# Where the first experts' weights are asked for: two 256 KB loads in each fifth convolution slot instead of one load beside nearly every block of x

## The chip, the cores and the metric

The kernel runs on one core of one Trainium2 chip. The metric is device time in microseconds (us). A core has engines that work side by side: TensorE (PE; its weight loads are listed apart as PEld), VectorE (DVE), ScalarE (ACT), GpSimd (POOL) and SyncE (SP). All loads and stores of this kernel are DMAs that SP issues in the order of its own instruction stream; sixteen DMA engines carry them out.

## What is computed

A convolution with weights that differ by token and head, followed by a soft mixture of experts. All data are float32.

```python
def _attn_ref(x, weight_gen):              # x [8, 3584, 192], weight_gen [8, 3584, 8 heads, 7 taps]
    w = softmax(weight_gen, axis=-1)       # over the 7 taps
    x_pad = concatenate([zeros(B, 6, D), x], axis=1)
    x_unf = x_pad[:, idx, :].reshape(B, S, 7, H, 24)
    return einsum('bshk,bskhg->bshg', w, x_unf).reshape(B, S, D)

def _moe_ref(x, phi, w1, w2):              # x [28672, 192], w1 [8, 192, 1024], w2 [8, 1024, 192]
    logits = x @ phi                       # 8 experts of 4 slots: 32 columns
    d = softmax over tokens (axis 0) of logits
    slot_input = (d.T @ x).reshape(8, 4, 192)
    slot_out[e] = relu(slot_input[e] @ w1[e]) @ w2[e]
    c = softmax over slots (axis 1) of logits
    return c @ slot_out
```

## The kernel before

The tokens are cut into 280 groups of 104. A **slot** `k` (0 to 69) is one call of `convs(k)`: the convolution of four groups on TensorE (64 matmuls of line 274), with ScalarE copying the result out of PSUM. Around it come six transposes per pair of groups (line 293) and, once per four slots, a **unit**: the logits (lines 345 and 349), their running maximum, the exponentials and the dispatch matmuls (line 425). VectorE, GpSimd and ScalarE turn the tap weights into the banded matrices (`band`) that the convolution multiplies with; they also do the softmax over slots (`soft`) for the tokens that are done.

After slot 69 there is a short chain: the rest of the last unit, then `hidden` (line 917, experts' first layer, reads `w1a_sb` and `w1b_sb`), `outputs` (line 934, second layer, reads `w2`), and then the output rows (line 996, copied at line 1005, stored at line 1012).

What SP loads, and when:

- `loadx` (line 170): a block of x, 32 partitions by 960 elements, 120 KB. Four of them make one x tile `t` (0 to 55) of five groups. `feed(k)` asks for tile `t + 4` in the slot in which tile `t` is used for the last time, `(5t + 4) // 4 == k`. So 480 KB of x are asked for in four slots of five, and none where `k` is a multiple of five.
- `loadw` (line 173): the tap weights (`wh`) of eight groups, 182 KB, once per two slots.
- `loadw1` (line 495): a piece of the first experts' weights, into `w1a_sb` or `w1b_sb`; these tiles have no other use before the output rows. A piece is 256 columns, 128 KB; with `n = 2` it is 512 columns, 256 KB. There are 48 pieces, 6.3 MB.
- `loadw2` (line 502): the second experts' weights, 256 KB each, into the memory of x tiles that are no longer needed.

`feed` only lists the operations. A planner (`model`, `times`) simulates the engines with the costs given in `op`, and the instructions are emitted in the order of the planned starts; on PE and SP the listed order is kept. Every DMA planned later than 24 us is held back by `paced`: SP waits for the PE instruction that stands at the same planned time. So SP's queue follows TensorE's progress.

Before the change, `feed` puts `loadw1` behind the x of a tile: 6 loads of 256 KB with tiles 3, 5, 7, 9, 12 and 14, then 30 loads of 128 KB with tiles 16 to 49 (seven tiles of eight), then 6 more of 128 KB beside the first `loadw2`.

Of the kernel before, what the change touches and what calls it, by code (L numbers as in the profile page):

```python
# [30 lines left out]
NS, E, SE, F = 32, 8, 4, 1024  # L31
# [2 lines left out]
TAIL = 4  # L34
PACED = 24.0
LEAD, LATE = 9, 4.6
WLATE, WPAIRS = 42, 12
FILL = 2
WGAP = 0.9
TR = 3 * 32 + T  # L40
# [22 lines left out]
def conv_soft_moe(ctx, tc, xh, wh, phi, w1a, w1b, w2a, w2b, out):  # L63
# [190 lines left out]
    def unit(p):  # L254
        return next((u, p - p0) for u, (p0, n) in enumerate(UNITS) if p < p0 + n)
# [257 lines left out]
    def op(eng, cost, reads, writes, f, *a, late=0.0, due=None):  # L513


        i = len(ops)
        preds = {writer[r] for r in (*reads, *writes) if r in writer}
        for r in writes:
            preds |= set(readers.get(r, ()))
            writer[r], readers[r] = i, []  # L520
        for r in reads:
            readers.setdefault(r, []).append(i)
        preds.discard(i)
        ops.append((eng, cost, late + 0.1 * (eng == "TE"), preds, due, f, a))
# [4 lines left out]
    def x_all(t):  # L529
        return [x_of(t, h) for h in range(4)]  # L530

    def loadxs(t, cost, late, hs=(0, 2, 1, 3)):
        for h in hs:
            op(SP, cost, [], [x_of(t, h)], loadx, t, h, late=late)
# [17 lines left out]
    VE, AC, PO, TE, SP = "VE", "AC", "PO", "TE", "SP"  # L552
# [113 lines left out]
    def feed(k):  # L666
        for c in range(3, NCH):
            if k == max(0, CH * c - 4):
                chain(c)
        for c in range(6, NCH):  # L670
            if k == CH * c - LEAD - (c > 9):
                op(SP, 0.5, [], [("w", c % NTAP, b) for b in range(CH)], loadw, c, late=LATE)
        for t in range(NSG):
            if (SGG * t + SGG - 1) // 4 == k:
                if t + NXS < NSG:
                    loadxs(t + NXS, 0.52, 3.0)
                else:
                    i = t + NXS - NSG
                    for j in range(WLATE + 3 * i, min(WLATE + 3 * (i + 1), 4 * (E + E // 2))):
                        op(SP, 0.5, [], [], loadw1, j)  # L680
                    freed = True
                    for j, (b, o, n) in enumerate(W2S):
                        if i == (W2B * b + o + n - 1) // XB:
                            op(SP, WGAP, [] if freed else x_all(t), x_all(t) if freed else [],
                               loadw2, j)
                            freed = False
                for j in range(WLATE):
                    n = 1 if j >= WPAIRS else 2 - j % 2 * 2
                    if n and 3 + j * 8 // 7 == t:
                        op(SP, 0.15 + 0.3 * n, [], [], loadw1, j, n)  # L690
        for c in range(NTAP, 6):
            if k == CH * c - 7 - c % 2:
                op(SP, 0.5, [], [("w", c % NTAP, b) for b in range(CH)], loadw, c, late=LATE)

    v = final - 1
    for k in range(SLOTS):
        u, i = unit(2 * k)[0], unit(2 * k)[1] // 2
        if u == final and i == 0:
            op(PO, 0.2, [], [("wide", b) for b in range(CH)]
               + [(*tm_of(x), j) for x in (k, k + 1) for j in range(2)], edges, [NTM], G)  # L700
        convs(k)
        if 0 < k < UP // 2 + 1:
            xposes(k - 1)
        feed(k)
        if i == 0 and u > 1:
            xposes(k - 2, k - 1)
        elif i == 1 and u > 0:
            slots(u - 1)
        elif i == 2 and u > 0:
            settle(u - 1)  # L710
            xposes(k - 2, k - 1)
        elif i == 3 and u > 0:
            ends(u - 1)
            saves(u - 1)
    k = SLOTS - 2
# [125 lines left out]
    for i in sorted(range(len(ops)), key=lambda i: (at[i], i)):  # L841
        if ops[i][5] is loadw2 and ops[i][6] in later:
            continue
        n = len(block.instructions)
# [356 lines left out]
```

## Time and profile before

| | |
|---|---|
| median of 3 timed runs | 287.76 us (286.5 to 290.84) |
| profiled execution, device time | 288.77 us |
| its span, first to last instruction | 286.6 us |
| TensorE busy | 256.9 us, 90% of the span |
| DMA engines busy (queue q1, data) | 73.6% of 16 engines' span |
| slots 0 to 69 | from 8 to about 210 us |
| last rows stored | from about 230 us to the end |

The page gives busy times per engine and a line of tenths in 40 slices. The slices show two parts: in the first three quarters TensorE is at 9 tenths in nearly every slice while the DMA engines stand at 5 to 9 tenths; in the last part the DMA engines are at 9 tenths and move about 420 GB/s. "Issue" as the reason of an idle time means that the engine waited for nothing that the profile shows. A DMA that SP issues is listed under SPq. Instruction fetches have DMA queues of their own (q8 and q14, "instruction").

### The profile page before, as it was taken

To read this page: it belongs to the slowest core of one execution; us is meant where nothing else is said; L and a number is where in the kernel's file an instruction comes from. 1 tells how busy PE (TensorE), PEld (TensorE's weight loads), DVE (VectorE), ACT (ScalarE), POOL (GpSimd) and SP (SyncE) were. 2 spreads that over 40 slices of the span, in tenths; PEclk is the share of its full clock that TensorE was granted. 3 is DMA by queue.
4 is the path that set the end of the run, shared out by engine and by line. 5 is a ranking of instruction groups with operands and counts; after the bars stand their busy time and mean duration, and the time that the engine had idled before them with its cause. 6 is when DMAs were issued, how large, how long until landed. Compare 5 with 4: busy or idle time off the path is not lost.

```text
span 286.6 us, 15079 instructions
## 1 busy us (share of the span) xinstructions
PE 256.9 (90%) x6520; PEld 200.9 (70%) x6520; DVE 211.6 (74%) x375; ACT 177.8 (62%) x296; POOL 161.5 (56%) x257
## 2 busy tenths in 40 slices
PE   8899989999999999999999999999999998899000
PEld 4688878888888988878898898898966743232000
DVE  8788888888867769978898899977357698954000
ACT  8887456765666577656776767757540089988100
POOL 9987848674567368488669798673312017530000
PEclk9999999999999999999999999999999999968655
DMA  5777976676765777758757667656889389999995
GB/s 173 213 200 222 255 226 195 179 217 195 230 200 150 217 222 213 208 164 237 203 178 209 196 205 231 187 177 191 258 284 301 111 316 417 420 429 427 419 429 225
DMA packets 28240, 69.69 MB, mean 243 GB/s; under 512 B 5648, under 2 KB 14992, under 8 KB 27024
## 3 DMA queue, kind: packets, MB, share of 16 engines
q1 hardware_dynamic: 28176, 68.75, 73.6%
q8 instruction: 51, 0.84, 1.2%
q14 instruction: 13, 0.11, 0.1%
HBM read 46.68 MB, written 22.04 MB: 240 GB/s over the span
## 4 chain that ended last, share of the span: by engine, by line
PE 78%; POOL 5%; DMA 4%; DVE 2%; ACT 2%; issue 2%; ACTq 0%; SPq 0%; POOLq 0%; DVEq 0%
PE ring L274 34%; PE ring L293 16%; PE acb L425 8%; PE two L996 5%; PE ls L345 4%; PE ls L349 4%; DMA out<-w1b_sb 2%; PE ring L917 2%; PE acb L373 2%; DMA out<-w1a_sb 1%; POOL big L441 1%; PE ring L934 1%; POOL LT L103 1%; ACT w1a_sb L1005 1%; POOL taps L205 1%
## 5 line engine op out<-in xcount | busy, mean ns | idle before, releaser
L274 PE MATMUL ring<-big,band 128*26 128x96 f32 x4480 | 109.4, 248 | 2.6 <-issue 1.3
L274 PEld LDWEIGHTS ring<-big,band 128*26 128x26 f32 x4480 | 99.3, 130 | 11.9 <-issue 6.4
L281 ACT COPY tm<-ring 128x768 f32<-128x768 f32 x68 | 54.4, 800 | 59.7 <-PE ring L274 59.6
L245 DVE STREAM_TRANSPOSE band<-wide 128x832 f32<-128x832 f32 x70 | 69.8, 1022 | 6.4 <-POOL wide L236 4.6
L293 PE MATMUL ring<-ident,tm 122*128 122x122 f32 x408 | 50.0, 272 | 0.8 <-issue 0.8
L293 PEld LDWEIGHTS ring<-ident,tm 122*128 122x128 f32 x408 | 43.7, 144 | 3.3 <-issue 0.8
L299 ACT COPY cm<-ring 128x624 f32<-128x624 f32 x68 | 44.0, 689 | 2.0 <-PE ring L293 2.0
L236 POOL TENSOR_TENSOR wide<-taps,sum 128x364 f32<-128x364 f32 x32 | 31.4, 982 | 16.8 <-DVE band L245 10.8
L205 POOL TENSOR_TENSOR taps<-taps,top 128x364 f32<-128x364 f32 x34 | 33.1, 976 | 8.8 <-DVE top L197 8.7
L221 POOL TENSOR_TENSOR si<-taps 128x208 f32<-128x208 f32 x34 | 21.7, 638 | 16.0 <-ACT taps L213 15.5
L197 DVE TENSOR_REDUCE top<-taps 128x52 f32<-128x364 f32 x34 | 27.8, 819 | 1.7 <-DMA taps<-wh 1.5
L425 PE MATMUL acb<-tm,dt 128*32 128x193 f32 x544 | 25.9, 328 | 0.5 <-issue 0.4
L103 POOL TENSOR_TENSOR LT<-LT,rm 128x576 f32<-128x576 f32 (+1 forms) x16 | 18.1, 1136 | 9.9 <-DVE rm L101 9.9
L115 POOL TENSOR_TENSOR LT<-LT,sm 128x576 f32<-128x576 f32 (+1 forms) x16 | 18.0, 1135 | 9.9 <-DVE sm L113 9.9
L996 PE MATMUL two<-cT,so 32*128 32x468 f32 (+4 forms) x136 | 20.8, 596 | 1.4 <-ACT w1a_sb L1005 0.8
L425 PEld LDWEIGHTS acb<-tm,dt 128*32 128x32 f32 x544 | 16.9, 110 | 4.1 <-issue 0.6
L355 DVE TENSOR_REDUCE mx<-ls 128x1 f32<-128x416 f32 x17 | 10.1, 592 | 12.8 <-PE ls L349 12.8
L213 ACT ACTIVATE taps<-taps 128x364 f32<-128x364 f32 (+1 forms) x36 | 18.1, 503 | 1.8 <-POOL taps L205 1.7
L227 DVE RECIPROCAL sum<-sum 128x52 f32<-128x52 f32 (+1 forms) x36 | 16.5, 457 | 3.2 <-POOL sum L223 3.0
L996 PEld LDWEIGHTS two<-cT,so 32*128 32x128 f32 x136 | 8.5, 196 | 12.6 <-ACT w1a_sb L1005 6.0
L1005 ACT COPY big<-two 128x936 f32<-128x936 f32 (+2 forms) x18 | 14.9, 910 | 0.8 <-PE two L996 0.7
L222 POOL TENSOR_TENSOR si<-si 128x104 f32<-128x104 f32 x34 | 13.9, 408 | 2.7
(140 smaller groups left out, 307.8 us busy)
## 6 DMA issues: line engine op xcount, KB each, us to landing
big<-xh SPq DMA_DIRECT2D x224, 120.0 KB, 3.4
out<-big SPq DMA_DIRECT2D x5, 1794.0 KB, 13.0
taps<-wh SPq DMA_DIRECT2D x35, 182.0 KB, 3.5
big<-w2a SPq DMA_DIRECT2D x16, 256.0 KB, 3.8
out<-w1b_sb SPq DMA_DIRECT2D x2, 1794.0 KB, 12.1
out<-w1a_sb SPq DMA_DIRECT2D x2, 1794.0 KB, 14.4
w1a_sb<-w1a SPq DMA_DIRECT2D x20, 128.0 KB, 3.5
w1b_sb<-w1b SPq DMA_DIRECT2D x16, 128.0 KB, 3.4
```

What stands on the lines that cost most here:

```text
L103: G.tensor_tensor(out=lt, in0=lt, in1=rms.pop(h).to_broadcast([128, n, NS]), op=ALU.subtract)
L197: V.tensor_reduce(out=row(m), in_=run(c, 0, KT).rearrange("p k s -> p s k"), axis=AX.X, op=ALU.max)
L205: eng.tensor_tensor(out=t, in0=t, in1=rows7(tops.pop((c, 0))), op=ALU.subtract)
L221: eng.tensor_tensor(out=fold, in0=run(c, 0, 4), in1=run(c, 4, 8), op=ALU.add)
L236: eng.tensor_tensor(out=dst, in0=raw[c % NTAP][:, 0:KT], in1=m.unsqueeze(1).to_broadcast([128, KT, n, T]), op=ALU.mult)
L245: V.transpose(bands[c % NBAND][:, b].rearrange("p b j l -> p (b j l)"), wide[:, b].rearrange("p b j -> p (b j)"))
L274: P.matmul(to, bands[g // 8 % NBAND][:, g // 4 % CH, :, i], xbd[:, place(t), :, b * GW : (b + 1) * GW].rearrange("p h (a i) -> p h a i", i ...
L281: copy(tms[tm_at(u)][:, pr + of.start : pr + of.stop, 1 : 2 * D + 1], cv[:, of, 0 : 2 * D])
L293: P.transpose(pt[:, j // 3, o : o + TR], tm[0:TR, pr + j // 3, 1 + o : 129 + o], ident[0:TR, 0:TR])
L299: copy(cm.rearrange("p (a i) (b j) -> p a (i b) j", i=3, j=T), pts["t", k][:, of, 0 : 3 * 128].rearrange("p a (i j) -> p a i j", j=32)[... ...
L425: P.matmul(ac[32 * q : 32 * q + 32], dt[:, g, :], tm[:, g // 2, o : o + D + 1], start=(g < 4), stop=(g + 4 >= 2 * n))
L996: P.matmul(pos[j][q // 2][m * half : m * half + m, q % 2, 0 : widths(g, n)[q]], of[32 * q : 32 * q + 32], cT[32 * q : 32 * q + 32, g0 : g0 ...
```

## The change

The lines of `feed` that tie `loadw1` to the x tiles are taken out, with their two constants. In their place, each slot `k` that is a multiple of five (the slots in which no x is asked for), from slot 10 to slot 65, lists two `loadw1` of 256 KB: 24 loads in 12 slots. The planner's cost for one is 0.75 us, as it was before for a load of 256 KB.

```diff
-WLATE, WPAIRS = 42, 12
...
                 else:
                     i = t + NXS - NSG
-                    for j in range(WLATE + 3 * i, min(WLATE + 3 * (i + 1), 4 * (E + E // 2))):
-                        op(SP, 0.5, [], [], loadw1, j)
                     freed = True
...
-                for j in range(WLATE):
-                    n = 1 if j >= WPAIRS else 2 - j % 2 * 2
-                    if n and 3 + j * 8 // 7 == t:
-                        op(SP, 0.15 + 0.3 * n, [], [], loadw1, j, n)
+        if k % 5 == 0:
+            for j in range(4 * (k // 5 - 2), 4 * (k // 5 - 1), 2):
+                if 0 <= j < 4 * (E + E // 2):
+                    op(SP, 0.75, [], [], loadw1, j, 2)
```

The order on TensorE is the same row for row. On VectorE, GpSimd and ScalarE some steps of `soft` change places with their neighbours. The large difference is on SP, at three places. (The kernel of the change has three lines less, so its line 169 is line 170 of before, and so on.)

SP near the start, before (`big<-xh` is x, `taps<-wh` the tap weights, `128x512` of `w1a` a 256 KB load):

```order
L170 DMA big<-xh 32x960 x8
L495 DMA w1a_sb<-w1a 128x512
L173 DMA taps_81<-wh 128x364
L170 DMA big<-xh 32x960 x4
L173 DMA taps_78<-wh 128x364
L170 DMA big<-xh 32x960 x4
L495 DMA w1a_sb<-w1a 128x512
L170 DMA big<-xh 32x960 x4
L173 DMA taps_79<-wh 128x364
L170 DMA big<-xh 32x960 x4
L495 DMA w1a_sb<-w1a 128x512
```

SP at the same place, after:

```order
L169 DMA big<-xh 32x960 x8
L172 DMA taps_81<-wh 128x364
L169 DMA big<-xh 32x960 x4
L172 DMA taps_78<-wh 128x364
L169 DMA big<-xh 32x960 x8
L172 DMA taps_79<-wh 128x364
L169 DMA big<-xh 32x960 x4
L172 DMA taps_80<-wh 128x364
L494 DMA w1a_sb<-w1a 128x512 x2
```

The first two w1 loads have left this stretch; the first pair of the change stands behind the same six x tiles as the third 256 KB load before.

SP in the middle of the convolutions, before (`128x256` of `w1a` or `w1b` is a load of 128 KB):

```order
L495 DMA w1b_sb<-w1b 128x256
L170 DMA big<-xh 32x960 x4
L495 DMA w1b_sb<-w1b 128x256
L173 DMA taps_78<-wh 128x364
L170 DMA big<-xh 32x960 x4
L495 DMA w1a_sb<-w1a 128x256
L170 DMA big<-xh 32x960 x4
L495 DMA w1a_sb<-w1a 128x256
L173 DMA taps_79<-wh 128x364
L170 DMA big<-xh 32x960 x4
L495 DMA w1a_sb<-w1a 128x256
L173 DMA taps_80<-wh 128x364
```

SP between the same tap loads, after:

```order
L494 DMA w1b_sb<-w1b 128x512 x2
L172 DMA taps_81<-wh 128x364
L169 DMA big<-xh 32x960 x8
L172 DMA taps_78<-wh 128x364
L169 DMA big<-xh 32x960 x8
L172 DMA taps_79<-wh 128x364
L494 DMA w1a_sb<-w1a 128x512 x2
L169 DMA big<-xh 32x960 x4
L172 DMA taps_80<-wh 128x364
```

Where every x tile had a w1 load beside it, two tiles now follow each other with a tap load at most, and the w1 loads come in pairs with a tap load next to them.

SP at the end of the convolutions, before:

```order
L170 DMA big<-xh 32x960 x8
L495 DMA w1b_sb<-w1b 128x256 x3
L502 DMA big<-w2a 128x512 x7
L495 DMA w1b_sb<-w1b 128x256 x3
L502 DMA big<-w2a 128x512 x9
L502 DMA big<-w2b 128x512 x8
```

and after:

```order
L169 DMA big<-xh 32x960 x8
L494 DMA w1b_sb<-w1b 128x512 x2
L169 DMA big<-xh 32x960 x16
L494 DMA w1b_sb<-w1b 128x512 x2
L501 DMA big<-w2a 128x512 x16
L501 DMA big<-w2b 128x512 x8
```

The last six w1 loads no longer stand between the loads of the second experts' weights.

## Rows read from the trace of the kernel before

**Rows 1.** Busy time, slots 2 to 69: us, busy (x instructions) per engine, PEclk, DMA share, GB/s.

```profile
13.40:209.60 196.20, 193.63 (x5707) 168.39 (x5707) 159.93 (x278) 129.26 (x226) 133.30 (x215) 1.00 0.71 206
```

**Rows 2.** TensorE's waits, 13.4 to 209.6 us, all of them: us, times, longest.

```profile
PE ring L274 <- issue: 1.3, 4, 0.4
PE ring L293 <- issue: 0.8, 1, 0.8
PE ring L274 <- DVE band L245: 0.5, 1, 0.5
PE acb L425 <- issue: 0.4, 1, 0.4
```

**Rows 3.** Chain that ended last, in order: start us, us, what.

```profile
21.70 0.70 PE ls L345 x8
...
33.73 0.70 PE ls L345 x6
...
46.54 0.70 PE ls L345 x8
...
92.54 0.70 PE ls L345 x8
...
103.87 0.70 PE ls L345 x8
...
208.22 0.70 PE ls L345 x8
...
228.76 0.60 PE two L996 x8
```

**Rows 4.** TensorE in order of time: start us, us, line, operation, [idle before <- releaser].

```profile
32.68 0.56 PE L274 MATMUL ring<-big,band 128*26 128x96 f32 x16 [0.33 <-issue]
...
37.53 0.68 PE L293 MATMUL ring<-ident,tm 122*128 122x122 f32 x5 [0.77 <-issue]
...
42.45 0.79 PE L274 MATMUL ring<-big,band 128*26 128x96 f32 x25 [0.24 <-issue]
...
124.21 0.41 PE L274 MATMUL ring<-big,band 128*26 128x96 f32 x9 [0.42 <-issue]
```

**Rows 5.** DMA queues, 13.4 to 209.6 us: packets, MB, share of 16 engines.

```profile
q8 instruction: 45, 0.74, 1.6%
```

**Rows 6.** DMA queues, 34.9 to 36.1 us.

```profile
q8 instruction: 1, 0.02, 6.0%
```

**Rows 7.** DMA queues, 33.0 to 34.9 us.

```profile
q1 hardware_dynamic: 242, 0.52, 92.9%
```

**Rows 8.** SP's issues in order of time, two stretches: start us, us, line, what.

```profile
25.02 1.25 SPq L495 DMA_DIRECT2D w1a_sb<-w1a  x1
...
32.30 0.35 SPq L495 DMA_DIRECT2D w1a_sb<-w1a  x1
...
38.39 0.37 SPq L495 DMA_DIRECT2D w1a_sb<-w1a  x1
...
119.03 0.37 SPq L495 DMA_DIRECT2D w1b_sb<-w1b  x1
119.57 0.35 SPq L173 DMA_DIRECT2D taps<-wh  x1
```

**Rows 9.** Busy time, 27 to 36 us, columns as in the first group.

```profile
27.00:36.00 9.00, 8.67 (x281) 7.77 (x273) 7.82 (x13) 4.93 (x8) 7.90 (x15) 1.00 0.92 257
```

**Rows 10.** DMA issues, 13.4 to 209.6 us: KB each, median us to landing.

```profile
big<-xh SPq DMA_DIRECT2D x208, 120.0 KB, 3.5
taps<-wh SPq DMA_DIRECT2D x31, 182.0 KB, 3.6
w1a_sb<-w1a SPq DMA_DIRECT2D x6, 256.0 KB, 4.0
```

**Rows 11.** DMA queues, 59.9 to 61.5 us.

```profile
q1 hardware_dynamic: 194, 0.44, 82.9%
q8 instruction: 1, 0.02, 5.0%
```

## The prediction

> **What bounds the kernel now.** I first read the busy times of the convolution part as one stretch. Of its 196.2 us TensorE is busy 193.6, while the DMA engines are busy 0.71 of the time [rows 1]. So loads as such do not bound this part; TensorE does, at a granted clock of 1.00, which is its upper level (2.4 GHz). Its waits come next. No entry in the list is a DMA of x, taps or w1; nearly all of it is "issue": 1.3 + 0.8 + 0.4 us in six pieces, in which TensorE waited for nothing that the profile shows [rows 2].
>
> The chain of work that ended last shows what those pieces cost. A unit of four slots starts with the logits of line 345. A quiet unit lasts 103.87 - 92.54 = 11.33 us. From the first listed start to the last, 208.22 - 21.70 = 186.52 us pass, which is 16 units; at 11.33 us they would take 181.28. So 5.24 us in all are lost, in some of the units [rows 3]. The first two are such: 12.03 us (0.70 too long) and 12.81 us (1.48 too long). TensorE in order of time shows the pieces in the middle of a run of equal matmuls, for instance 0.77 us up to 37.53 and 0.42 us up to 124.21 [rows 4]. The first unit holds one piece (up to 32.68), the second two, so one costs 0.70 to 0.74 us of unit time, more than its idle in most rows (0.24 to 0.77). I call it a stall. The remaining three of the six waits come after 103.87 us, where nine units take 208.22 - 103.87 = 104.35 us, 2.38 more than 9 x 11.33: 0.79 each. The four units from 46.54 to 92.54 lose 46.00 - 45.32 = 0.68 us without a listed wait of TensorE.
>
> What are they? In this part the instruction queue q8 carries 45 packets [rows 5], while TensorE starts 5707 matmuls and 5707 weight loads [rows 1]: 11414 / 45 = 254 instructions per packet. So q8 is TensorE's code, a block each 4.4 us. A packet runs between 34.9 and 36.1 us [rows 6], the stall ends at 37.53. In the 1.9 us before that packet the data queue kept the DMA engines busy to 92.9% [rows 7]. My reading: behind much data a code block is fetched late, and TensorE runs dry.
>
> The Trainium skill, "Runtime: NRT & Kernel Launch", section "Instruction fetch mechanics", says that code is refilled in 16 KiB blocks of 256 instructions (the trace agrees: 254) and that crossing a block costs a DMA step that is "mostly hidden". Here six of 45 are not. By the rule taken strictly the stalls are something else and the change leaves the time as it is; that is the first rival below.
>
> **The change, part by part.** The bytes stay: 6.3 MB of w1. Only when they are asked for changes, and in which size. TensorE's order is the same, so every term is a stall more or less.
>
> *How full a slot is.* A slot lasts 11.33 / 4 = 2.83 us. At a DMA share of 0.92 the queues moved 257 GB/s [rows 9], so full engines move 280 GB/s here, or 0.79 MB per slot. Demands by the sizes issued [rows 10]: x 4 x 120 KB = 0.49 MB, taps 0.19 MB in every second slot, w1 0.13 or 0.26 MB. Before: x, taps and a 128 KB w1 make 0.81 MB (1.02 of a slot); with a 256 KB w1 0.94 MB (1.19); x and w1 0.62 (0.79). After: x and taps 0.68 (0.85), x alone 0.49 (0.62); the fifth slot with its pair 0.52 (0.66), with taps 0.71 (0.90). No slot is overfull any more.
>
> *First stretch, to 46.5 us.* Before, 256 KB loads are issued at 25.02, 32.30 and 38.39 us [rows 8], and the first two stalls lie within 8 us of the first two. In the change both are gone and the first pair stands where the third load was. I take two stalls away, 0.70 + 0.74 = 1.44 us; the third, up to 42.45, stays, since a pair is now close to it.
>
> *After 46.5 us.* 0.68 + 2.38 = 3.06 us are lost there. Ahead of the stall at 124.21, w1 and taps are issued back to back (119.03, 119.57) between x tiles [rows 8]. The change takes w1 out of the x slots, but puts 0.52 MB in a row once in five slots (14.2 us, against a code block each 4.4 us). I count half of the loss as gone: 1.53 us.
>
> *New stalls beside the twelve pairs.* Until the x loads end, the trace shows no two w1 loads in a row. The bound below is none (a pair fills 0.66 to 0.90 of its slot). The bound above is one stall at each pair: 12 x 0.70 = 8.4 us. I take one, 0.70 us, nearer the lower bound, since three of the six 256 KB loads [rows 10] come after the three just named, and the four units from 46.54 us on show no stall.
>
> *Work that the change costs at nothing.* (a) 24 issues instead of 42: SP's issues take 0.35 to 0.38 us where nothing holds them [rows 8], and SP waits for TensorE anyway. (b) A 256 KB load of w1 landed 4.0 us after its issue [rows 10]; the last pair is asked for in slot 65, four slots or 11 us before the last slot ends, and w1 is first read after that. (c) x behind a pair: 0.52 MB at 280 GB/s hold it up by 1.9 us; x is asked for one tile turn ahead of three others, 3.75 slots or 10.6 us before use, against 3.5 us of landing. Taps are asked for still earlier. If that cover were gone, each late x would cost TensorE up to 1.9 us. (d) The steps of `soft` that change places on the other engines: they delay a `band` by one such step at most; the waits list names bands with 0.5 us, once [rows 2]. (e) At the end, six w1 loads leave the stretch of the w2 loads. The chain from 208.22 to the first output rows at 228.76 [rows 3] names no load, so I give this nothing; the stores behind it keep their length.
>
> *Sum.* -1.44 - 1.53 + 0.70 = -2.3 us. Against the profiled execution: 288.8 - 2.3 = 286.5 us (span 286.6 - 2.3 = 284.3). That execution is 1.0 us above the median of the runs shown, so against the median, 287.76 - 2.3 = 285.5 us.
>
> **The rivals.**
>
> *No change.* The stalls come when they come, or the load does not decide. For it: a code packet between 59.9 and 61.5 us met 82.9% of data load and no stall followed [rows 11]. Against it: the first two stalls lie where the slots are fullest (1.19). Time: 287.8 us. Another page would give the same: the Trainium skill, "DMA: Bandwidth & Descriptors", section "Queues, rings and completion order", says that a DMA engine takes turns between its queues packet by packet, so that code would wait for one data packet and not for a backlog; the trace neither shows nor excludes that, as the rows name no queue depth.
>
> *Nearly all stalls go.* If the overfull slots alone cause them, 4.6 (the six) to 5.24 us are won: 282.5 to 283.2 us. Against it: 0.90 of a slot stays, and 82.9% is not far from 92.9%.
>
> *Slower: a pair starves code.* Two loads of 256 KB in a row put 0.52 MB before a code block that comes then; with taps beside them 0.71 MB, or 2.5 us of transfer, more than half of the 4.4 us between blocks. If each pair stalls TensorE once: 8.4 us more and at most 5.2 less, 291.0 us. It is slower from the eighth stall at pairs on (5.24 / 0.70 = 7.5), and by over 2% (5.8 us) only if a pair costs (5.8 + 5.2) / 12 = 0.92 us each.
>
> *The change doesn't do what it says*: the planner could have moved the pairs to other places. SP's order shows them between taps and x as described, so I give this none.
>
> **How the numbers follow.** Some stalls go (1 to 3.5 us won): 50%. Nearly all go: 15%. No change within 1 us: 22%. Slower by 1 to 5.7 us: 10%. Slower by more: 3%. The likeliest gives **285.5 us**. The range leaves out most of the slower cases (above 1.4 us of loss) and the last third of "nearly all go": **282.8 to 289.2 us**. A measurement of this kernel can tell about 2% (5.8 us) from no change. Faster by that is more than all the time lost in the convolutions (5.24 us), so only an error in the reading gives it: 0.04. Slower by that: 0.03. Within: 0.93.
>
> **What would show it.** In the profile after, the units of the first stretch should last 11.3 to 11.6 us, where they lasted 12.03 and 12.81; the data queue should stay below nine tenths there; TensorE's "issue" waits should fall from 2.5 us to about 1.5 us in three or four pieces; the output part should keep its length and start 2 us earlier. The prediction is wrong if the pieces stay as many with the load evened out (then load is not the cause), if they gather behind the pairs, or if TensorE begins to wait for x or taps.

## The result: the change costs 0.8%, and where the time went

The changed kernel takes 289.67 us (median of 14 timed runs, 288.78 to 292.12), the kernel before, timed beside it, 287.72 us (14 runs, 286.5 to 291.12). The ratio is 1.0076, 95% interval 1.0049 to 1.0103. On another chip the same two kernels later gave 290.44 against 288.78 us, ratio 1.0032 (0.9996 to 1.0068). So it is slower by 0.3 to 0.8%, where 0.8% faster was forecast, and the time lies outside the range. The ratios here leave out runs that are over 1.5% above the fastest of the same kernel, so they can differ a little from the quotient of the medians.

The profiled execution took 291.1 us, its span is 289.1 us, 2.5 more than the span of before. Lines of the kernel after are one lower up to about line 500 (L273 is L274 of before).

Busy times of the changed kernel by stretch: us, busy (x instructions) of TensorE, its weight loads, VectorE, ScalarE, GpSimd, then the granted clock, DMA share, GB/s:

```profile
13.40:46.60 33.20, 33.20 (x1014) 28.73 (x1018) 29.36 (x45) 22.59 (x41) 25.38 (x50) 1.00 0.74 218
46.60:209.60 163.00, 158.18 (x4628) 137.42 (x4624) 129.68 (x234) 105.76 (x184) 107.84 (x165) 1.00 0.67 201
```

```profile
13.40:212.00 198.60, 193.78 (x5706) 167.88 (x5706) 159.66 (x278) 129.15 (x226) 133.68 (x215) 1.00 0.69 205
```

The same matmuls (5706 against 5707) are busy for the same time as before (193.78 against 193.63 us), at the same granted clock of 1.00; but they need 198.60 us where they needed 196.20 [rows 1]. TensorE never pauses up to 46.6 us. It pauses later, 4.8 us in 163, with the DMA engines less busy than before. So it is no lack of bandwidth on average.

TensorE's waits, 13.4 to 212 us, all of them (us, times, longest):

```profile
PE ring L273 <- issue: 3.3, 6, 0.9
PE acb L372 <- DVE top L196: 0.9, 1, 0.9
PE ls L344 <- ACT taps L212: 0.6, 1, 0.6
PE ring L273 <- DVE band L244: 0.5, 1, 0.5
```

"Issue" was 2.5 us in six pieces before [rows 2] and is 3.3 us in six pieces. Two entries are new, with 1.5 us together. They name VectorE and ScalarE, but what the two matmuls read was written over a microsecond before they started at 71.86 and 117.37 us: `mq` until 70.62, `cm` until 116.02 (start us, us, what):

```profile
70.40 0.22 DVE L356 TENSOR_SCALAR mq<-acb,mx 128x4 f32<-128x4 f32 x1
...
114.71 1.31 ACT L298 COPY cm<-ring 128x624 f32<-128x624 f32 x2
```

So I count them as stops of the same kind; the last section has a second reason.

The chain that ended last, at the starts of units (start us, us, what):

```profile
21.78 0.70 PE ls L344 x8
33.11 0.70 PE ls L344 x8
44.59 0.70 PE ls L344 x8
56.95 0.70 PE ls L344 x7
...
104.24 0.70 PE ls L344 x8
117.37 0.91 PE ls L344 x8
...
210.86 0.70 PE ls L344 x8
```

The first two units take 11.33 and 11.48 us where they took 12.03 and 12.81 [rows 3]: this gain came. Then it turns. The third unit takes 12.36 us, the one from 104.24 even 13.13. From 21.78 to 210.86 us the 16 units take 189.08 us, which is 7.80 above 16 x 11.33 (5.24 before). The rest of the span keeps its length: 289.1 - 210.86 = 78.2 us, before 286.6 - 208.22 = 78.4.

Where TensorE stops (start us, us, line, [idle before <- releaser]):

```profile
53.68 0.39 PE L273 MATMUL ring<-big,band 128*26 128x96 f32 x4 [0.65 <-issue]
...
71.86 0.36 PE L372 MATMUL acb<-mq,sel 128*128 128x5 f32 x2 [0.86 <-DVE top L196]
...
89.63 0.39 PE L273 MATMUL ring<-big,band 128*26 128x96 f32 x7 [0.78 <-issue]
...
107.80 0.37 PE L273 MATMUL ring<-big,band 128*26 128x96 f32 x2 [0.85 <-issue]
```

And what SP issues ahead of the first of them (start us, us until the last of the group is issued, what, how many):

```profile
48.01 0.35 SPq L172 DMA_DIRECT2D taps<-wh  x1
48.45 1.78 SPq L169 DMA_DIRECT2D big<-xh  x4
50.32 0.85 SPq L494 DMA_DIRECT2D w1a_sb<-w1a  x2
51.55 0.88 SPq L172 DMA_DIRECT2D taps<-wh  x1
54.35 2.13 SPq L169 DMA_DIRECT2D big<-xh  x3
```

The pair goes out 0.09 us after the four x of the *previous* slot, its two loads less than half a microsecond apart. Nothing follows for about 2 us after the taps at 51.55. So the pair does not lie in the middle of the slot without x; it lengthens the burst ahead of it. From 48.01 to 52.43 us SP asks for 0.19 + 0.49 + 0.52 + 0.19 = 1.39 MB, where 4.4 us at 280 GB/s (the full engines of [rows 9]) move 1.24. A packet of code comes into this burst; it runs between 51.15 and 52.4 us, from 51.18 on (queues in that stretch):

```profile
q1 hardware_dynamic: 136, 0.29, 72.3%
q8 instruction: 1, 0.02, 4.4%
```

That packet took 0.88 us (4.4% of 16 engines for 1.25 us), so it was over at 52.06; TensorE stands still from 53.03 to 53.68. Not every stop has a pair ahead of it. Those at 89.63, 107.80 and 126.01 us come 8.5 to 14.5 us behind the last pair (issued at 81.13, 97.06 and 111.53 us); a load of w1 took 3.4 to 4.2 us to land (medians). The first of these pairs:

```profile
81.13 0.85 SPq L494 DMA_DIRECT2D w1a_sb<-w1a  x2
```

So this trace does not show pair by pair what makes a stop.

### The profile page after: what moved, and what is told of

It is laid out like the page before. It is cut to its first block, busy times and chain, and to the rows that moved or that the text cites. A ratio compares the mean times of both kernels' runs of the same rounds, so it can differ in the third digit from the quotient of the medians.

```text
span 289.1 us, 15044 instructions
## 1 busy us (share of the span) xinstructions
PE 255.1 (88%) x6520; PEld 199.8 (69%) x6520; DVE 211.3 (73%) x375; ACT 177.4 (61%) x296; POOL 161.9 (56%) x257
## 4 chain that ended last, share of the span: by engine, by line
PE 76%; DVE 5%; POOL 5%; issue 3%; ACT 2%; ACTq 0%; DVEq 0%; POOLq 0%
PE ring L273 34%; PE ring L292 16%; PE acb L424 8%; PE two L993 4%; PE ls L344 4%; PE ls L348 4%; PE ring L914 2%; PE acb L372 2%; POOL big L440 1%; PE ring L931 1%; ACT w1a_sb L1002 1%; DVE big L1002 1%; POOL LT L102 1%; DVE cT L482 1%; POOL taps L204 1%
## 5 line engine op out<-in xcount | busy, mean ns | idle before, releaser
L273 PE MATMUL ring<-big,band 128*26 128x96 f32 x4480 | 109.9, 248 | 4.7 <-issue 3.3
L273 PEld LDWEIGHTS ring<-big,band 128*26 128x26 f32 x4480 | 99.3, 130 | 14.6 <-issue 8.3
L993 PE MATMUL two<-cT,so 32*128 32x468 f32 (+4 forms) x136 | 19.5, 553 | 1.8 <-ACT w1a_sb L1002 0.8
L344 PE MATMUL ls<-cm,phi_sb 128*32 128x416 f32 x136 | 15.0, 513 | 0.6 <-ACT taps L212 0.6
```

Source lines behind the costliest of these rows:

```text
L273: P.matmul(to, bands[g // 8 % NBAND][:, g // 4 % CH, :, i], xbd[:, place(t), :, b * GW : (b + 1) * GW].rearrange("p h (a i) -> p h a i", i ...
L344: P.matmul(lp[32 * blk : 32 * blk + 32, lo:hi, :, 0:T], phi_sb[:, 0, :], cm[:, lo:hi, 0:3:2, blk, :], start=True, stop=False)
L993: P.matmul(pos[j][q // 2][m * half : m * half + m, q % 2, 0 : widths(g, n)[q]], of[32 * q : 32 * q + 32], cT[32 * q : 32 * q + 32, g0 : g0 ...
```

## The experiments

Theory A at the start: a pair costs when it comes just ahead of a fetch of code, so its place relative to the code block decides. Rivals: the amount of w1 in a slot, the size of one load, or something without relation to w1. A stall's size in one execution scatters (see the end), so what follows rests on the ratios, and losses of one trace (first to last unit, less 16 x 11.33 us) only support them.

### Where the pair stands relative to the code

The loads are taken out of the planner's list. In the loop that emits the instructions, TensorE's instructions are counted, and at chosen counts a load is emitted that waits for that instruction. 256 counts are a block of code.

```diff
-        if k % 5 == 0:
...
-                    op(SP, 0.75, [], [], loadw1, j, 2)
...
+            for j in new:
+                code[0] += one
+                while plan and code[0] * 1.0122 + 10 >= plan[0][0]:
+                    _, w, m = plan.pop(0)
...
+                    loadw1(w, m)
...
+PLAN = [(256 * i + 165, 4 * n + m, 2) for n, i in enumerate((7, 11, 13, ...)) for m in (0, 2)]
```

The second kernel has `+ 300` for `+ 165`, which is about 2 us later. The third puts single loads of 256 KB there, `(256 * i + 300, 2 * n, 2)` in 24 blocks.

> The changed kernel with the same twelve pairs of 256 KB loads, but each pair held back by the TensorE instruction that stands about 0.8 us ahead of the start of a code block's fetch (every 256 TensorE instructions one block; twelve odd-numbered blocks between the 7th and the 41st). Theory A (a pair in front of a code fetch delays the code and TensorE runs dry): a stall of 0.7 to 1.0 us at most of the twelve blocks, so the 16 units lose 8 to 12 us over 16 x 11.33 us, where the changed kernel lost 7.8 and the kernel before 5.2; time 290 to 294 us. Rival B (the place among the code blocks does not matter, 0.5 MB in one piece costs the same anywhere): loss as in the next run, within 1 us of the changed kernel, 289 to 290.5 us.

> The same twelve pairs, each 135 TensorE instructions (about 2.1 us) later, so that it is asked for when the code block's packet has begun or is done, and has 2.8 us until the next block's fetch. Theory A: hardly a stall at the pairs; the 16 units lose 0 to 3 us, time 282.5 to 285.5 us, 6 to 9 us less than the run with the pairs ahead of the code. Rival B: no difference between the two, both 289 to 290.5 us.

> 24 single loads of 256 KB, each behind the start of a code block's fetch, in 24 of the blocks 5 to 43. Theory A: half the data behind each fetch, and 3.6 us until the next one; 0 to 2 us lost in the 16 units, time 282.5 to 285 us, the fastest of these. Rival B: as the other runs, 287 to 290 us, since the same 6.3 MB pass through the same part.

Measured: pairs ahead of the fetch 290.44 us, ratio 1.0066 (1.0023 to 1.0109); behind it 290.84 us, 1.0103 (1.0011 to 1.0194); singles 293.17 us, 1.0150 (1.0051 to 1.0250, four timed runs, as for the one before). In the traces the units lose 5.88, 5.60 and 6.08 us, where theory A had 8 to 12, 0 to 3 and 0 to 2. All are slower than the kernel before, and no better than the changed kernel. The place relative to the fetch makes no difference that shows: theory A falls in this form.

### Without the loads

All 24 loads are asked for behind the last slot's x (`if k == SLOTS - 1` for `if k % 5 == 0`).

> No w1 load during the convolutions: all 24 loads of 256 KB stand behind the last slot, so the experts' first layer waits for them (the end of the kernel is late by 10 us or more, which is not the question). It shows what x and taps alone do to TensorE. Theory A: 0 to 1 us lost in the 16 units. Rival C (x tiles that follow each other without a w1 load between them delay the code themselves): 4 us lost or more, as in the kernel before.

One execution: 299.87 us, since the second part now waits for w1. But the convolutions show what the loads cost. Chain, first and last unit, and all of TensorE's waits:

```profile
21.70 0.70 PE ls L344 x8
...
204.96 0.70 PE ls L344 x8
```

```profile
PE ring L273 <- issue: 0.6, 1, 0.6
PE ring L273 <- DVE band L244: 0.5, 1, 0.5
PE ring L424 <- DVE taps L405: 0.5, 1, 0.5
```

The units lose 204.96 - 21.70 - 181.28 = 1.98 us, more than theory A's 0 to 1 and well below rival C's 4. It is the least of all 17 profiled executions; the others lose 3.1 to 9.0. So w1 goes with most of the loss: about 7.80 - 1.98 = 5.8 us in the changed kernel (8.98 - 1.98 = 7.0 in its second profiled execution), and 5.24 - 1.98 = 3.3 in the kernel before. Each figure is from one execution, and one kernel scatters by about 3 us (see the end), so the 3.3 is not shown.

### The same places, another size

Four loads of 128 KB for each pair of the changed kernel; and the kernel before with all its loads beside x of 256 KB, or all of 128 KB.

```diff
-            for j in range(4 * (k // 5 - 2), 4 * (k // 5 - 1), 2):
+            for j in range(4 * (k // 5 - 2), 4 * (k // 5 - 1)):
...
-                    op(SP, 0.75, [], [], loadw1, j, 2)
+                    op(SP, 0.375, [], [], loadw1, j, 1)
```

```diff
-WLATE, WPAIRS = 42, 12
+WLATE, WPAIRS = 42, 42
```

(and `42, 0` in the third).

> The changed kernel with the same 512 KB of w1 in the same fifth slots, but as four loads of 128 KB (rows of 1 KB) where there were two of 256 KB (rows of 2 KB). Theory D (what delays the code is the size of one load: all its rows on a DMA engine go ahead of the code packet, 8 rows of about 0.10 us at 256 KB and 8 of about 0.055 us at 128 KB): stalls become few, the 16 units lose 3 to 4.5 us where the changed kernel lost 7.8 and the kernel without w1 in the convolutions 2.0; the time is 1.0 to 1.5% below the changed kernel's, that is 0.990 to 0.998 of the kernel before. Rival F (512 KB in one slot is what counts, in whatever pieces): as the changed kernel, 1.005 to 1.010 of the kernel before.

> The kernel before with its w1 loads in their old places beside the x tiles, but all of the first 42 pieces as loads of 256 KB (21 loads, beside every second x tile from the fourth on) in place of 6 of 256 KB and 30 of 128 KB. Theory D: slower than before as the changed kernel is, 1.005 to 1.012; loss in the 16 units 7 to 9 us. Rival F (0.5 MB in one slot): the bytes per slot never exceed 256 KB of w1, so as before, 0.997 to 1.003, loss 4 to 6 us.

> The kernel before with all w1 loads of 128 KB: the six early loads of 256 KB become twelve of 128 KB beside the x tiles from the fourth on. Theory D: the three stalls of the first 25 us go, loss in the 16 units about 3 to 3.5 us (before 5.2), 0.992 to 0.996 of the kernel before. Rival F, and the first reading by how full a slot is: x, taps and w1 of 128 KB still overfill a slot slightly, and the later stalls stay; loss 4.5 to 5.5 us, 0.998 to 1.002.

Measured: four of 128 KB in a row 290.29 us, 1.0044 (1.0010 to 1.0079); 256 KB beside x 290.83 us, 1.0061 (1.0034 to 1.0088); 128 KB beside x 288.08 us, 0.9978 (0.9948 to 1.0007). The last two differ in nothing but whether a load is 128 KB beside seven in eight x tiles or 256 KB beside half as many, and their intervals are far apart: this is the clearest result. Bytes, and the mean load over all slots, are the same in both. But a load of 256 KB also doubles the w1 of its slot (by the prediction's sums 1.19 of a slot with x and taps, where 128 KB make 1.02), and its rows are 2 KB instead of 1 KB; the pair of kernels doesn't separate these. Cutting the pair into pieces that SP issues in a row does not help by itself. So neither theory holds alone: D had four of 128 KB at 0.990 to 0.998, F had 256 KB beside x at 0.997 to 1.003. The units lose 6.47, 5.86 and 3.32 us in the traces.

### Held back to the pause

Theory G: the pair costs because it stands directly behind the x run, when the data queue is still full. The loads wait for TensorE again, now counted from the last x ahead of the slot without x: the pair 2.5 us behind it and 1.1 us apart; or four of 128 KB, about 0.65 us apart; or all 48 loads of 128 KB singly, two in each pause and one behind the x run of slots without taps. As an example, the entries of the second pause (count, load, quarters) in the first two kernels:

```diff
+PLAN = [..., (2631, 4, 2), (2697, 6, 2), ...]
...
+PLAN = [..., (2580, 4, 1), (2621, 5, 1), (2661, 6, 1), (2702, 7, 1), ...]
```

> The changed kernel with the same two loads of 256 KB in each fifth slot, but SP holds the first until TensorE is some 2.5 us behind the release of the last x of the slot before, and the second 1.1 us later, so that both go out in the middle of the pause without x instead of right behind the x run. Theory 'directly behind the x run' (the pair costs because the data queue is still full when it is added): the units lose 2 to 4 us instead of 7.8, the ratio to the kernel before is 0.990 to 0.998. Rival 'amount in a fifth slot' (512 KB in one lump keep the queue full past the next code block wherever in the pause they are asked for): the units lose 5.5 to 8 us, ratio 1.003 to 1.010.

> As the kernel with the pair held back, but the 512 KB as four loads of 128 KB, each held until TensorE has gone on by some 0.65 us, so that they go out evenly over the pause. Theory 'directly behind the x run': the units lose 2 to 3.5 us, ratio 0.988 to 0.997, and below the four loads of 128 KB right behind the x run (1.0044). Rival 'amount in a fifth slot': 5 to 7 us lost, ratio 1.003 to 1.008, like those four.

> All 48 loads of 128 KB apart from each other: two in each pause of a fifth slot, 1.2 us apart, and one behind the x run of each slot that loads no convolution weights. Theory 'directly behind the x run': half of the loads are there again, if only 128 KB each; loss 3 to 4.5 us, ratio 0.994 to 1.002, no better than the four held back. Rival 'amount in a lump' (only how much is asked for at once counts, the place does not): the best of the three, loss 2 to 3.3 us as in the kernel with 128 KB beside every x tile (0.9978), ratio 0.990 to 0.998, and better than both kernels with 512 KB in the pause.

> The changed kernel once more, on the same chip as the three with loads held back, as their yardstick: 1.005 to 1.010 of the kernel before by every theory, with 6 to 8 us lost in the units.

SP's issues of the pair held back, then of the four, these from the second execution that was profiled (start us, us, what):

```profile
79.52 0.35 SPq L173 DMA_DIRECT2D taps<-wh  x1
81.77 0.99 SPq L495 DMA_DIRECT2D w1a_sb<-w1a  x2
83.06 1.25 SPq L170 DMA_DIRECT2D big<-xh  x3
```

```profile
80.12 0.35 SPq L173 DMA_DIRECT2D taps<-wh  x1
80.92 2.74 SPq L495 DMA_DIRECT2D w1a_sb<-w1a  x4
```

In the first, 1.9 us without an issue lie ahead of the pair, as was meant; over the twelve pairs it is 0.4 to 3.5 us. Measured: the pair held back 289.80 us, 1.0037 (1.0013 to 1.0062), beside 1.0032 for the changed kernel on the same chip. Theory G falls for the pair: the pause ahead of it gives nothing. Four of 128 KB held back 288.94 us, 0.9993 (0.9964 to 1.0022); singles 289.22 us, 0.9998 (0.9965 to 1.0030). The three with loads of 128 KB apart from each other, these two and 128 KB beside x, are level with the kernel before, though their loads stand in quite different places. None reaches the 0.990 to 0.998 that 'amount in a lump' had for the singles. The units lose 5.94 us with the pair, 3.12 with the four, 7.43 with the singles. All waits of TensorE in the convolutions with the four spaced ones (again from the second execution, the one on the chip of the next section):

```profile
PE ring L274 <- issue: 1.0, 3, 0.5
PE ring L274 <- DVE band L245: 0.5, 1, 0.5
```

Its units start at 21.69 and 206.21 us, a loss of 3.24 us.

### Amount at once, size of a request, or length of a row

A load of 256 KB is one request, 256 KB at one moment, and rows of 2 KB instead of 1 KB. Four loads of 128 KB in a row, all at the place of the pair held back, change the request and the row, not the amount. Four spaced loads of half the partitions with rows of 2 KB keep the planned times and the bytes of the four held back.

```diff
+PLAN = [..., (2631, 4, 1), (2631, 5, 1), (2631, 6, 1), (2631, 7, 1), ...]
```

```diff
-        SY.dma_start(to[:, e, f], w[:, e, f])
+        p = slice(0, 128) if n < 3 else slice(64 * (n - 3), 64 * (n - 2))
+        SY.dma_start(to[p, e, f], w[p, e, f])
```

> The place of the pair held back (first issue 2.5 us behind the release of the last x), the same 512 KB, but as four loads of 128 KB straight behind each other (SP issues them 0.46 us apart). Theory 'size of one request' (256 KB asked for by one instruction are what delays the code): as the four spaced loads held back, ratio 0.995 to 1.002. Rival 'lump' (512 KB within 2 us, in whatever pieces): as the pair held back and the four directly behind the x run, 1.003 to 1.007.

> The kernel with four spaced loads of 128 KB held back, but each load takes half the partitions with rows of 2 KB, as the loads of 256 KB have them, instead of all 128 with rows of 1 KB; bytes and times of issue are unchanged. Theory 'size of one request' or 'lump': 0.995 to 1.002, as with rows of 1 KB. Rival 'length of a row' (a code packet's turn comes later the longer the packets of the data queue are): 1.003 to 1.008, as the loads of 256 KB.

> The four spaced loads of 128 KB held back once more, on the same chip as the two kernels that are compared with it: 0.996 to 1.003 by every theory.

> 128 KB beside every x tile, none of 256 KB, once more: 0.995 to 1.001 of the kernel before by every theory; it shows whether this version is faster than both kernels or level with the one before.

Measured on one chip: four in a row 289.17 us, 1.0038 (1.0004 to 1.0072); rows of 2 KB 289.96 us, 1.0043 (1.0001 to 1.0086); the four spaced, with rows of 1 KB, 288.06 us, 0.9984 (0.9946 to 1.0022); 128 KB beside x 288.69 us, 0.9989 (0.9954 to 1.0024). The units lose 5.75, 7.62, 3.24 and 6.23 us in the traces.

The size of a request is not what counts: four requests in a row cost what two of twice the size cost in that place (1.0037), and what four cost behind the x run (1.0044). Against the spaced loads on the same chip the four in a row are at 1.0047 (1.0011 to 1.0083), the rows of 2 KB at 1.0067 (1.0022 to 1.0112). Two cautions go with this. First, "spaced" and "in a row" differ less than planned: the spaced four go out over 2.5 us on average in both their traces, the four in a row over 1.75, and 23 and 20 of the 36 steps between spaced loads are below 0.55 us. Second, the rows of 2 KB are the most spaced of the three (3.1 us) and cost at least as much. So amount at once does not explain them; but that kernel also uses half the partitions per load, and the rows of x (3.8 KB) are longer still in every kernel.

Every version that loads w1 during the convolutions in rows of 2 KB, but for six pieces at most, comes out slower than the kernel before (1.0032 to 1.0150), whether in pairs or single. Of the five with rows of 1 KB alone, the two with four loads in a row are slower (1.0044 and 1.0038) and three are level. That a burst costs, and that rows of 2 KB cost, are thus both likely, and no run separates them fully. No version is faster than the kernel before beyond its interval; the spaced loads and those of 128 KB beside x are level with it. On one chip the four spaced took 288.94 us against 290.44 of the changed kernel.

## Why the prediction was wrong, point by point

**What bounds the part.** Right. TensorE is busy for the same 193.8 us, and a loss is a pause of TensorE. That w1 is behind most pauses fits the kernel without these loads, 1.98 us lost instead of 5.24, but that is one execution of each. Of the signs named beforehand, "the pieces stay as many" came true (six and six); yet the w1 loads are a cause, as 256 KB against 128 KB beside x shows.

**First stretch, -1.44.** Right in direction: the two units became 2.03 us shorter. That this was the price of the 256 KB loads is not shown. The kernel with 256 KB beside x has the same loads in the same places of this stretch, and its two units lose 45.06 - 21.72 - 22.66 = 0.68 us, where the kernel before lost 2.18:

```profile
21.72 0.70 PE ls L345 x8
...
45.06 0.70 PE ls L345 x8
```

So a good part of the 1.44 us was luck of the one execution that was read.

**After 46.5 us, -1.53 and +0.70.** Wrong, and this is the failed part of the sum. The units from the third boundary on lost 3.06 us before and lose 7.65 us now (210.86 - 44.59 less 14 x 11.33): +4.6 where the two terms gave -0.8. With the first stretch, -2.0 + 4.6 = +2.6 us, which is the 2.5 us of the span. The kernel without w1 splits the two terms: from its third boundary on (44.51 us) it loses 204.96 - 44.51 - 158.62 = 1.83 us. By that, 1.2 of the 3.06 us went with the old loads, near the 1.53 of the forecast, and the new loads cost 5.8 us where "New stalls beside the twelve pairs" had 0.70. This term is the step that failed.

**The step behind it: "How full a slot is".** I averaged demand over a slot of 2.83 us and found the slot with a pair 0.66 to 0.90 full, and from that took the bound of no stall. The waits are not a matter of that average. The changed kernel overfills no slot and is slower than the kernel that did. With the same bytes in the same slots, on one chip each, two loads of 256 KB held back are at 1.0037 and four of 128 KB at 0.9993; four in a row at 1.0038 and four further apart at 0.9984. What has to be counted is how a slot's bytes are asked for: in a row or apart, and in which rows. (256 KB beside x against 128 KB is no test of the average, since by it too the slots with 256 KB are overfull.) The prediction passed over its own price: in the first stretch it blamed 256 KB loads for 0.70 us each, and then added 24 of them for 0.70 us in all. By the loss of the kernel without loads, the twelve pairs cost 5.8 us, 0.49 each on average: closer to my upper bound (0.70 each) than to the 0.06 that I took.

**Where the pairs stand.** I gave no chance to the planner moving them, since the order of SP shows them between taps and x. The order was right and the time was not: the planner gives a load that depends on nothing the first moment at which SP is free, so all twelve pairs go out 0.1 to 0.2 us behind the x or taps issued before them. It was a real error of reading, yet not the cause: the pair in the middle of the pause costs as much.

**The rivals.** "Slower: a pair starves code" had the direction, with 13% in all; its 291.0 us is 1.3 above the measured 289.67. "No change" is excluded on the first chip. The page "DMA: Bandwidth & Descriptors" of the Trainium skill, section "Queues, rings and completion order", would have code wait for one data packet and not for a backlog. Spaced loads and loads in a row consist of the same packets and were 0.9984 and 1.0038: the runs speak against that reading here, if not beyond doubt, as the two differ in place by about a microsecond too.

**What cost nothing.** Right: no wait for x or w1 in the list, and the rest of the span is 78.2 us against 78.4. The two new entries that name VectorE and ScalarE (0.9 and 0.6 us) read like stops of the same kind, as said above.

**What stays open.** How much of the cost is the burst and how much the rows of 2 KB. And the last link, a code packet that is late behind a burst, is argued from the traces: every one of the 69 "issue" stops between 14 and 205 us, in all executions, ends 2.2 to 3.5 us after a code packet starts. But the packet at 51.15 to 52.4 us was over a microsecond before TensorE stopped, three stops had no pair near them, and no run changed the code's own queue, so it isn't shown.

## What to carry to other kernels

A prefetch that nothing waits for can still cost time in a part that TensorE bounds: look at how it is asked for, not at the mean load of a stage alone. Here loads of 128 KB in rows of 1 KB, apart from each other, were level with the kernel before, and larger or bunched ones were slower. Check in the trace where a load goes out, as a planner puts one that depends on nothing right behind the last burst. And where a trace already puts a price on an operation, let the sum try that price for each new one, or say what makes the new ones cheaper.

## What the runs showed that was not expected

The same program loses a different amount in each execution. 128 KB beside x, profiled twice, first and last unit each time:

```profile
22.36 0.70 PE ls L345 x8
...
206.96 0.70 PE ls L345 x8
```

```profile
22.34 0.70 PE ls L345 x8
...
209.85 0.70 PE ls L345 x8
```

That is a loss of 3.32 and of 6.23 us by the same instructions, so the 5.24 us that the prediction divided up were one draw of a quantity that varies by a few microseconds. And with no w1 in the convolutions the DMA share fell to 0.62, yet one pause of 0.6 us named "issue" remained.

The stops stand at fixed instructions. Stretches from one stop to the next, first of the changed kernel, then of the kernel before (columns as in the busy times above):

```profile
53.67:71.85 18.18, 17.32 (x506) 14.82 (x506) 14.72 (x23) 11.26 (x18) 11.33 (x18) 1.00 0.62 186
71.85:89.62 17.77, 17.00 (x505) 15.02 (x506) 13.02 (x23) 10.29 (x19) 9.30 (x17) 1.00 0.71 208
```

```profile
37.52:124.20 86.68, 85.88 (x2529) 74.75 (x2529) 70.91 (x123) 55.20 (x95) 53.56 (x87) 1.00 0.70 204
124.20:159.45 35.25, 34.57 (x1011) 30.05 (x1011) 30.88 (x55) 23.88 (x42) 28.79 (x42) 1.00 0.70 202
```

Some 506 matmuls and 506 weight loads lie between two stops, or a multiple of that (2529 is five times 506, 1011 twice). That is 1012 instructions, four of the code packets with 254 each. Over all 17 executions, 60 of the 69 "issue" stops stand at nine instructions that are the same in every kernel, and the other nine stand a whole number of packets away. The stop that names VectorE at 71.86 us is in the same row. This is the strongest sign that the stops come from the code: the program fixed where TensorE stopped, and the loads only which of these places did, and for how long. In the kernel with the pairs ahead of the fetch, six of the twelve stood ahead of such a place, and only two of these six places stopped. Why it is every fourth packet, no run shows.
